# Fourier layer: the middle row by ScalarE and GpSimd, and 64 columns' high and low parts in one stationary operand

## The chip, the cores and the metric

The kernel runs on one core of a Trainium2 chip. A core has a matrix engine (TensorE, PE in the profile, with its weight loads apart as PEld), a vector engine (VectorE, DVE), a scalar engine (ScalarE, ACT), GpSimd (POOL), and DMA queues, most of them fed by SyncE (SP). Each engine works through its own list of instructions in order, and a semaphore holds an instruction back until what it reads is there. Matrix products land in PSUM, in eight banks of 512 fp32 columns; everything else lies in SBUF. The metric is the device time of one execution in microseconds (us), and the median of several runs stands for a kernel.

## The reference

Two equal layers of attention and of Fourier mixing, on 2048 tokens of 640 channels in fp32, 32 heads of 20:

```python
x = A_x
x = x + attention(layernorm(x), wqkv, wo)
x = x + fourier(layernorm(x))
x = x + attention(layernorm(x), wqkv, wo)
x = x + fourier(layernorm(x))

def fourier(x, seq_re, seq_im, hid_re, hid_im):
    a = einsum("bsd,ed->bse", x, hid_re)
    b = einsum("bsd,ed->bse", x, hid_im)
    return einsum("ts,bse->bte", seq_re, a) - einsum("ts,bse->bte", seq_im, b)
```

The matrices are the cosines and sines of the discrete Fourier transforms over 2048 tokens (seq) and 640 channels (hid). Their symmetries let the kernel fold rows and columns: it adds and subtracts mirrored tokens and channels first and then multiplies a quarter of the matrices. Row S/2 of the result, the middle row, falls out of that folding and is computed by itself, with weights of plus and minus one for each token.

## The kernel before

A layer has four stages: QKV projections, the attention sweep (by far the longest), Project, and Fourier. The change touches the last two.

**High and low parts.** A fp32 value is split into a high part in the reduced format fp32r and a low part, the rest (`split`, L85 to L91: the high part by ScalarE, the low part, a subtraction, by VectorE). A product of two such values takes three TensorE passes: high by high, high by low, low by high (`three`, L93 to L98).

**Project** (`Project.run`, L1161) goes over p = 0 to 7, pairs of token tiles. For each p: the output projection (`product`, PSUM tile py, VectorE adds it to the residual xr with a row sum), `moments` (L1104: the mean on GpSimd, squares xsq on ScalarE, then six small GpSimd operations that end in the statistics nb, and VectorE's channel folds g), `scale` (the three ScalarE operations of na, L1133 to L1138) and `normal` (L1144). `normal(p)` multiplies and adds by VectorE (f, L1150); for p = 2, 3, 6, 7 it also folds the tokens by two VectorE operations (L1155) and splits the result into xn, the operand of the Fourier stage, for q = 0, 1, 2, 3 (two tiles each). `LAG` says at which p a `normal(k)` is written: q = 0 at p = 4, q = 1 at p = 5, and q = 2 and 3 behind the last `moments`. There is no planner here: each engine's order is that in which the code is written.

**Fourier** (`Fourier.run`, L1416) makes 16 steps m in the order 0, 1, 4, 5, 2, 6, 3, 7, 8 to 15. `accumulate(m)` multiplies xn (stationary) by the sequence weights chl (moving, 512 columns) into three banks, one for each entry of `FOLDS[ri]`, nine passes in all; step m works on q = m % 4, and ri = (m // 4) % 2 tells the real from the imaginary half. The last step of four may add a three-row corner product (L1308). Then `turn` (L1311) splits the three banks into u. The weights chl are split by `parts` (L1285 to L1296) some steps ahead, in six tiles: those of the steps m = 0, 1, 4, 5, 2 and 6 in Project, those of m = 3, 7, 8, 9 behind the last `normal`, the rest later. `hidden` (L1371) multiplies u by the hidden weights wh, which `weights` (L1211) loads by SP and splits.

**The middle row** (`middle`, L1316). After m = 6 TensorE multiplies the weights mids by xn of q = 0 to 2 (18 passes of 322 or 320 columns into pmid), after m = 7 by q = 3 (6 passes). Three VectorE operations on one partition (L1331, L1333, L1336) bring the sum into um, in the tile c3raw, and add the corner term. After m = 9 six one-column products turn um into columns (pturn), and after m = 10 these are multiplied by the hidden weights.

## Time and profile before

| | us |
|---|---|
| median of 3 runs | 2438.72 (2437.7 to 2438.84) |
| span of the profiled execution | 2438.4 |
| TensorE busy | 2417.5 (99%) |
| ScalarE busy | 2115.4 (87%) |
| VectorE busy | 1008.6 (41%) |
| GpSimd busy | 546.6 (22%) |
| first row of m = 0, second layer, from the span's start | 2361.80 |

The profiled execution has no time of its own beside its span, which lies inside the range of the runs. A row of the trace reads: start in us, length in us, engine, line of the code, operation, the tile written, an arrow, the tiles read, then shapes (partitions x elements), the count, and in brackets how long the engine stood idle before, and what ended that. In the table of stretches the columns behind the window are its length and the busy time of PE, PEld, DVE, ACT and POOL with the number of instructions, then the granted TensorE clock (1.00 is full speed), the DMA engines' busy share and GB/s. TensorE's matmuls are pipelined and overlap, so the distance between two starts is what one costs. The two layers have the same rows here.

### The profile page before, as it was taken

The numbers are of one execution on the slowest core, as the hardware profiler recorded it, in microseconds if no ns is written. First come the engines' busy times: TensorE is split into PE (matmuls) and PEld (weight loads), VectorE is DVE, ScalarE is ACT, GpSimd is POOL, SyncE is SP. The second block draws the span as 40 slices with busy tenths as digits, with TensorE's granted clock in tenths as the row PEclk, the third lists the DMA queues.
The fourth block names the chain that finished last, engine by engine and source line by source line (L and its number), as shares of the span: only waits on it lengthen the run. The fifth ranks groups of instructions, "written<-read, shape, count | busy, mean of one in ns | idle before, by whom it ended". The sixth has DMA issues, their size and how long they took to land. (4 is left out here: it accounts for less than half of the span.)

```text
span 2438.4 us, 43899 instructions
## 1 busy us (share of the span) xinstructions
PE 2417.5 (99%) x16264; PEld 1163.5 (48%) x16264; DVE 1008.6 (41%) x2272; ACT 2115.4 (87%) x2426; POOL 546.6 (22%) x1072
## 2 busy tenths in 40 slices
PE   9999999999999999999999999999999999999998
PEld 8544444543333332339884444454433333333596
DVE  7244442234343333427773444323333232333275
ACT  5699998899999999995457999988999999999862
POOL 3022221112212222115341212211211111222143
PEclk9999999999999999999999999999999999999999
DMA  6324231223222225318573332312221322252265
GB/s 211 121 88 127 84 111 54 77 68 113 72 94 90 88 89 161 102 39 295 187 233 104 108 101 93 110 54 70 82 81 57 92 63 69 57 154 78 76 242 198
DMA packets 130803, 267.88 MB, mean 110 GB/s; under 512 B 30976, under 2 KB 55328, under 8 KB 130580
## 3 DMA queue, kind: packets, MB, share of 16 engines
q1 hardware_dynamic: 90964, 162.51, 20.4%
q0 software_dynamic: 39616, 102.47, 13.3%
q8 instruction: 131, 2.15, 0.4%
q14 instruction: 92, 0.75, 0.1%
HBM read 174.63 MB, written 84.31 MB: 106 GB/s over the span
## 5 line engine op out<-in xcount | busy, mean ns | idle before, releaser
L613 ACT ACTIVATE e<-psc 128x1024 f32<-128x1024 f32 x2048 | 1917.3, 1060 | 108.0 <-PE psc L610 97.7
L621 PE MATMUL acc<-e,v 128*32 128x512 f32 x8192 | 1030.0, 600 | 0.4 <-DVE of L628 0.4
L610 PE MATMUL psc<-stq,stk 62*128 62x512 f32 x4096 | 743.1, 445 | 3.1 <-ACT e L613 2.2
L610 PEld LDWEIGHTS psc<-stq,stk 62*128 62x128 f32 x4096 | 334.5, 184 | 699.7 <-ACT e L613 546.0
L621 PEld LDWEIGHTS acc<-e,v 128*32 128x32 f32 x8192 | 210.2, 108 | 410.8 <-issue 378.1
L103 PE MATMUL pqk<-xt,wqk 128*128 128x512 f32 x1200 | 322.4, 410 | 1.2 <-DVE xt L91 0.7
L642 POOL DMA_DIRECT2D o<-oh x256 | 131.1, 521 | 826.0 <-DVE oh L637 814.3
L88 DVE CAST hl<-pqk 128x512 fp32r<-128x512 f32 x64 | 44.3, 692 | 599.4 <-PE pqk L103 599.4
L103 PEld LDWEIGHTS pqk<-xt,wqk 128*128 128x128 f32 x1200 | 215.1, 189 | 85.6 <-issue 38.0
L103 PE MATMUL pv<-wv,xt 128*128 128x320 f32 x960 | 151.7, 313 | 0.0
L103 PEld LDWEIGHTS pv<-wv,xt 128*128 128x128 f32 x960 | 141.0, 188 | 13.5 <-issue 10.2
L628 DVE STREAM_TRANSPOSE of<-acc 128x512 f32<-128x512 f32 x64 | 45.8, 715 | 225.7 <-PE acc L621 225.7
L642 POOL DMA_DIRECT2D o<-ot x256 | 128.2, 509 | 1.5 <-DVE c L88 0.6
L272 POOL DMA_DIRECT2D scrk<-hl x40 | 28.0, 700 | 398.0 <-DVE hl L91 253.6
L272 POOL DMA_DIRECT2D scrq<-hl x40 | 28.8, 720 | 367.9 <-DVE hl L91 237.6
L96 PE MATMUL py<-wo,o 128*128 128x320 f32 x320 | 101.0, 316 | 0.0
L891 DVE TENSOR_REDUCE far<-cq 128x1 f32<-128x512 f32 (+5 forms) x169 | 98.6, 584 | 5.7
L97 PE MATMUL py<-wo,o 128*128 128x320 f32 x320 | 98.7, 308 | 0.0
L98 PE MATMUL py<-wo,o 128*128 128x320 f32 x320 | 98.7, 308 | 0.0
L895 DVE TENSOR_TENSOR cq<-cq 128x512 f32<-128x512 f32 (+4 forms) x166 | 96.4, 581 | 3.8 <-DMA cq<-in_nat_seq_dram 3.2
L311 DVE COPY v<-pv 128x320 f32<-128x320 f32 x32 | 15.7, 490 | 161.2 <-PE pv L103 161.2
L281 DVE TENSOR_REDUCE top<-pn 32x1 f32<-32x512 f32 x50 | 33.7, 677 | 76.8 <-PE pn L280 76.6
(212 smaller groups left out, 1779.4 us busy)
## 6 DMA issues: line engine op xcount, KB each, us to landing
cq<-in_nat_seq_dram POOLq DMA_DIRECT2D x64, 512.0 KB, 5.2
scrq<-hl POOLq DMA_DIRECT2D x40, 512.0 KB, 3.8
scrk<-hl POOLq DMA_DIRECT2D x40, 512.0 KB, 3.2
stq<-scrq SPq DMA_DIRECT2D x256, 80.0 KB
stk<-scrk SPq DMA_DIRECT2D x128, 160.0 KB
o<-o SPq DMA_DIRECT2D x32, 384.0 KB
stq<-scrq SPq DMA_DIRECT2D x256, 40.0 KB
stk<-scrk SPq DMA_DIRECT2D x128, 80.0 KB
```

The lines of the kernel that those rows point to most:

```text
L96: PE.matmul(out_ap, ah, bh, start=start, stop=False)
L97: PE.matmul(out_ap, ah, bl, start=False, stop=False)
L98: PE.matmul(out_ap, al, bh, start=False, stop=stop)
L103: yield lambda i=i, j=j, k=k: PE.matmul(out_ap, a[i], b[j], start=dc == 0 and k == 0, stop=dc == ND - 1 and k == 2)
L272: G.dma_start(s.scr["qk"[k]][c * 128:(c + 1) * 128, :, tb * 512:(tb + 1) * 512], hl.bitcast(F32))
L610: PE.matmul(p[:, i], s.k[g, kc // 8, j][r, kc % 8 * 128:(kc % 8 + 1) * 128], s.q[g, qb, j][r], start=True, stop=True)
L613: A.activation(e, p, AF.Exp, scale=SCALE)
L621: PE.matmul(s.acc[32 * j:32 * j + 32], s.a.v[kc][:, v0:v0 + 32], s.e[n, j // 2][:, j % 2], start=kc == 0, stop=kc == NT - 1, skip_group_ch ...
L628: V.transpose(t0.rearrange("p b c -> p (b c)"), s.acc)
L642: G.dma_start(s.o[k, h * DH:(h + 1) * DH, qb * 512:(qb + 1) * 512], hl[k][32 * j:32 * j + DH])
L891: V.tensor_reduce(to, x, op=OP.max, axis=AX.X, apply_absolute_value=True)
L895: V.tensor_tensor(y, x, y, op=op)
```

## The change

Three things are changed.

1. The folds of the imaginary half are cut at 449 and 576 in place of 449 and 575, so that the last piece has 64 columns. A tile of xn now holds the high parts of 640 columns, then the low parts with those of the last 64 columns first. The high and the low part of these 64 columns so stand side by side and make one stationary operand of 128 columns (`both`). In the four steps of each half with ri = 1, `accumulate` multiplies it by the high part of chl in one pass into 128 rows, and the high part by chl's low part in a second pass into 64 rows: two passes for three. The corner product of that piece moves ahead of its last pass. The rows of high and low stay apart through `turn`, and `hidden` adds them up over 128 partitions, with the 64 rows of hidden weights loaded twice (two DMAs on SP in place of one). The low part of xn is written by two VectorE operations, of 64 and 576 columns, in place of one.
2. The products of mids and xn after m = 6 and m = 7 are gone. In their place `weigh` stands at the end of `normal`: ScalarE multiplies the two folded tiles of each q by the weight of each partition (321 and 319 columns), and GpSimd adds q = 1, 2 and 3 to the sum (128 x 640). The six one-column products sum over 128 partitions.
3. The corner term of the middle row is added on one partition by one VectorE operation in `edge_sum(1)`, at p = 6; the tile mids is half as large and its split is gone.

The order on ScalarE at the end of Project, where na is that of p = 7, xn and the weighed rows those of q = 3, and chl the weights of m = 3, 7, 8 and 9, stood so before:

```order
L1136 ACTIVATE na<-g,nb,ars 128x321
L1137 ACTIVATE na<-g,nb,ars 128x2
L1138 ACTIVATE na<-g,zero,ars 128x319
L90 ACTIVATE xn<-fold_24675 128x640
L90 ACTIVATE xn<-fold 128x640
L1291 ACTIVATE chl<-craw 128x512 x4
```

and on the same engine at the same place it now reads:

```order
L1137 ACTIVATE na<-g,nb,ars 128x321
L1138 ACTIVATE na<-g,nb,ars 128x2
L1139 ACTIVATE na<-g,zero,ars 128x319
L1161 ACTIVATE xn<-fold_24675 128x640
L1161 ACTIVATE xn<-fold 128x640
L1286 ACTIVATE c3raw<-fold_24675,zero,mid 128x321
L1286 ACTIVATE c3raw<-fold,zero,mid 128x319
L1317 ACTIVATE chl<-craw 128x512 x4
```

The two weighing operations of q = 3 stand between xn and the four chl; those of q = 0, 1 and 2 stand behind their xn in the same way.

On GpSimd, between p = 4 and p = 5 (nb are the statistics of p = 4, mean and sumsq those of p = 5), the order was:

```order
L1128 TENSOR_TENSOR nb<-ars 128x1
L1129 TENSOR_SCALAR nb<-nb 128x1
L1130 TENSOR_SCALAR nb<-ars 128x1
L1110 TENSOR_TENSOR mean<-rowsum 128x2
L1111 TENSOR_SCALAR mean<-mean 128x2
L1115 TENSOR_SCALAR sumsq<-sumsq 128x2
```

and on GpSimd it now is:

```order
L1129 TENSOR_TENSOR nb<-ars 128x1
L1130 TENSOR_SCALAR nb<-nb 128x1
L1131 TENSOR_SCALAR nb<-ars 128x1
L1290 TENSOR_TENSOR um<-um 128x640
L1111 TENSOR_TENSOR mean<-rowsum 128x2
L1112 TENSOR_SCALAR mean<-mean 128x2
L1116 TENSOR_SCALAR sumsq<-sumsq 128x2
```

The addition of q = 1 stands ahead of the mean of p = 5. Those of q = 2 and 3 stand behind nb of p = 7, where GpSimd had nothing until `hidden`.

On TensorE, from the last passes of m = 6 to the first of m = 3, there stood (the line of dots leaves out 16 more passes into pmid):

```order
L96 MATMUL pacc<-chl,xn 65x512
L97 MATMUL pacc<-chl,xn 65x512
L98 MATMUL pacc<-chl,xn 65x512
L96 MATMUL pmid<-xn,mids 66x322
...
L98 MATMUL pmid<-xn,mids 66x320
L96 MATMUL pacc<-chl,xn 128x512
```

and TensorE now has there:

```order
L99 MATMUL pacc<-chl,xn 127x512
L1332 MATMUL pacc<-chl,xn 128x512
L1334 MATMUL pacc<-chl,xn 64x512
L97 MATMUL pacc<-chl,xn 128x512
L98 MATMUL pacc<-chl,xn 128x512
```

The first pass of m = 3 comes right behind the two passes of m = 6's last piece.

```diff
@@ -33,7 +33,8 @@
 HD = D // 2
 TOL = 2.0 ** -32
 
-FOLDS = (((0, 128), (128, 128), (256, 65)), ((321, 128), (449, 126), (575, 65)))
+FOLDS = (((0, 128), (128, 128), (256, 65)), ((321, 128), (449, 127), (576, 64)))
+WIDE = (1, 2)
 
 
 @with_exitstack
@@ -1032,7 +1033,7 @@
     class Project:
         def __init__(s, att, src, dst):
             s.att, s.src, s.dst, s.w, s.raw = att, src, dst, {}, {}
-            s.sum = {}
+            s.sum, s.both = {}, {}
             s.oh, s.x, s.xn, s.rs, s.f, s.g, s.nb, s.na = {}, {}, {}, {}, {}, {}, {}, {}
 
             s.begun, s.parts = set(), [lambda n=n, i=i: s.begin(n, i) for n in range(5) for i in range(2)]
@@ -1154,9 +1155,14 @@
             for k, op in enumerate((OP.add, OP.subtract)):
                 V.tensor_tensor(t[k], s.f[p - 2], f, op=op)
             for k in range(2):
-                xn = s.next.keep(f"xn{2 * q + k}", [2, D], F32R, "xn")
-                s.xn[q, k] = [xn[:, 0], xn[:, 1]]
-                split(xn[:, 0], xn[:, 1], t[k])
+                xn = s.next.keep(f"xn{2 * q + k}", [2 * D], F32R, "xn")
+                cut = FOLDS[1][2][0]
+                s.xn[q, k], s.both[q, k] = [xn[:, :D], xn[:, 2 * D - cut:]], xn[:, cut:]
+                A.activation(xn[:, :D], t[k], AF.Copy)
+                for to, cols in ((D, slice(cut, D)), (2 * D - cut, slice(cut))):
+                    V.tensor_tensor(xn[:, to:to + cols.stop - (cols.start or 0)], t[k][:, cols],
+                                    xn[:, cols].bitcast(F32), op=OP.subtract)
+            s.next.weigh(q, t)
 
         def run(s):
             s.ot[2] += s.heads(s.room, 2, (1,))
@@ -1208,6 +1214,10 @@
             s.loads = [0, 2, 1] + list(range(3, 8))
             pr.next = s
 
+        @staticmethod
+        def deep(ri, c):
+            return FOLDS[ri][c][1] * (2 if (ri, c) == WIDE else 1)
+
         def weights(s, k):
             ri, c = divmod(k, 3)
             k0, n = FOLDS[ri][c]
@@ -1216,11 +1226,12 @@
                 s.w[ri, c] = s.late(f"wh{k}", [2, HD + 2], F32R, "wh")
                 s.raw["w", k] = s.late(f"raw{(k + 1) % 2}", [D], F32, "whraw")[:, :HD + 2]
                 r0 = k0 - HD * ri
-                nc.sync.dma_start(s.raw["w", k][:n], hid[ri, r0:r0 + n, :HD + 2])
+                for a in range(0, s.deep(ri, c), n):
+                    nc.sync.dma_start(s.raw["w", k][a:a + n], hid[ri, r0:r0 + n, :HD + 2])
 
             def parts():
-                w = s.w[ri, c]
-                split(w[:n, 0], w[:n, 1], s.raw["w", k][:n], vector=True)
+                w, d = s.w[ri, c], s.deep(ri, c)
+                split(w[:d, 0], w[:d, 1], s.raw["w", k][:d], vector=True)
 
             return load, parts
 
@@ -1260,14 +1271,29 @@
                 A.activation(h, e, AF.Copy)
                 return
             V.tensor_tensor(l, e, h.bitcast(F32), op=OP.subtract)
+            m = s.um[0:1, :HD + 1]
+            V.scalar_tensor_tensor(m, e[:, :HD + 1], s.mm[0:1, 0:1], m, op0=OP.mult, op1=OP.add)
             nc.sync.dma_start(s.e3[1:2, 0].bitcast(F32), h.bitcast(F32))
             nc.sync.dma_start(s.e3[2:3, 0].bitcast(F32), l.bitcast(F32))
 
+        def weigh(s, q, t):
+
+            if q == 0:
+                x = s.keep("xn7", [2, D], F32, "um")
+                s.um, s.term = x[:, 0], x[:, 1]
+            to = s.room[:, :D] if q == NQ - 1 else s.term if q else s.um
+            for ri, cols in enumerate((slice(0, HD + 1), slice(HD + 1, D))):
+                A.activation(to[:, cols], t[ri][:, cols], AF.Identity, scale=s.midraw[:, ri, q // 2, q % 2:q % 2 + 1],
+                             bias=zero)
+            if q:
+                um = s.um if q == 1 else to if q == NQ - 1 else s.pr.room("xsq", [D], F32, "um")
+                G.tensor_tensor(um, s.um, to, op=OP.add)
+                s.um = um
+
         def mids(s):
-            x = s.keep("mids", [4, 80], F32R, "mids")
+            x = s.keep("mids", [2, 80], F32R, "mids")
             V.memset(x.bitcast(F32), 0.0)
-            s.mid, s.uc = [x[:, 0], x[:, 1]], [x[:, 2], x[:, 3]]
-            split(s.mid[0][:, :8], s.mid[1][:, :8], s.midraw.rearrange("p r k i -> p (r k i)"), vector=True)
+            s.uc = [x[:, 0], x[:, 1]]
 
 
         ORDER = (0, 1, 4, 5, 2, 6, 3, 7) + tuple(range(8, 16))
@@ -1301,44 +1327,39 @@
                 s.acc[ri] = [bank(f"b{3 * ri + c}", [128, 512], "pacc") for c in range(3)]
             ch, last = s.c[m], q == NQ - 1
             for c, (k0, n) in enumerate(FOLDS[ri]):
-                three(s.acc[ri][c][:n], [x[:, k0:k0 + n] for x in s.pr.xn[q, ri ^ tb]], (ch[:, 0], ch[:, 1]),
-                      q == 0, last and ri != tb)
+                x, stop = s.pr.xn[q, ri ^ tb], last and ri != tb
+                if (ri, c) == WIDE:
+                    fs = [lambda first, end: PE.matmul(s.acc[ri][c], s.pr.both[q, ri ^ tb][:, :2 * n], ch[:, 0],
+                                                       start=first, stop=end),
+                          lambda *_: PE.matmul(s.acc[ri][c][:n], x[0][:, k0:k0 + n], ch[:, 1], start=False, stop=False)]
+                    if last and ri == tb:
+                        fs.append(lambda *_: s.corner(tb, ri, c, False))
+                    for f in fs[::-1] if last else fs:
+                        f(q == 0, last)
+                else:
+                    three(s.acc[ri][c][:n], [y[:, k0:k0 + n] for y in x], (ch[:, 0], ch[:, 1]), q == 0, stop)
             if last and ri == tb:
-                for c, (k0, n) in enumerate(FOLDS[ri]):
-                    PE.matmul(s.acc[ri][c][:n], s.e3[0:3, 0, k0:k0 + n], s.c3[0:3, tb * 512:(tb + 1) * 512],
-                              start=False, stop=True)
+                for c in range(3):
+                    if (ri, c) != WIDE:
+                        s.corner(tb, ri, c, True)
+
+        def corner(s, tb, ri, c, stop):
+            k0, n = FOLDS[ri][c]
+            PE.matmul(s.acc[ri][c][:n], s.e3[0:3, 0, k0:k0 + n], s.c3[0:3, tb * 512:(tb + 1) * 512], start=False, stop=stop)
 
         def turn(s, tb, ri):
             u = s.u[tb, ri] = [s.own(f"u{(4 * tb + 2 * ri + k) % 6}", [3, 512], F32R, "u") for k in range(2)]
-            for c, (_, n) in enumerate(FOLDS[ri]):
+            for c in range(3):
+                n = s.deep(ri, c)
                 split(u[0][:n, c], u[1][:n, c], s.acc[ri][c][:n])
 
         def middle(s, step):
 
             if step == 0:
-                s.um = s.room[0:1, :2 * HD + 2]
-                s.pm = [bank(f"b{6 + ri}", [128, 512], "pmid")[:66] for ri in range(2)]
-            if step < 2:
-                for ri, (k0, n) in enumerate(((0, HD + 2), (HD, HD))):
-                    p = s.pm[ri][:, :n]
-                    for q in (range(NQ - 1), (NQ - 1,))[step]:
-                        j = NQ * ri + q
-                        three(p, [s.mid[k][:, j:j + 66] for k in range(2)],
-                              [x[:, k0:k0 + n] for x in s.pr.xn[q, ri]], q == 0, q == NQ - 1)
-                    if step == 0:
-                        continue
-                    if ri == 0:
-                        V.scalar_tensor_tensor(s.um[:, :HD + 1], s.e3[0:1, 0, :HD + 1].bitcast(F32), s.mm[0:1, 0:1],
-                                               p[0:1, :HD + 1], op0=OP.mult, op1=OP.add)
-                        V.scalar_tensor_tensor(s.um[:, :HD + 1], s.e3[0:1, 1, :HD + 1].bitcast(F32), s.mm[0:1, 0:1],
-                                               s.um[:, :HD + 1], op0=OP.mult, op1=OP.add)
-                    else:
-                        V.tensor_copy(s.um[:, HD + 1:D], p[0:1, 1:])
-            elif step == 2:
                 p = bank("b6", [128, 6], "pturn")
                 for ri in range(2):
                     for c, (k0, n) in enumerate(FOLDS[ri]):
-                        PE.matmul(p[:n, 3 * ri + c:3 * ri + c + 1], s.um[:, k0:k0 + n], one[0:1], start=True, stop=True)
+                        PE.matmul(p[:n, 3 * ri + c:3 * ri + c + 1], s.um[:, k0:k0 + n], one, start=True, stop=True)
                 for ri in range(2):
                     for c, (_, n) in enumerate(FOLDS[ri]):
                         i = 3 * ri + c
@@ -1377,7 +1398,8 @@
             if t == NQ and s.dst is out:
                 s.end(0)
             for ri in range(2):
-                for c, (_, n) in enumerate(FOLDS[ri]):
+                for c in range(3):
+                    n = s.deep(ri, c)
                     three(p[ri], [s.u[t // NQ, ri][k][:n, c, o:o + 128] for k in range(2)],
                           [s.w[ri, c][:n, k] for k in range(2)], c == 0, c == 2)
                 if final:
@@ -1429,8 +1451,8 @@
                     s.parts(i + s.AHEAD)
                 elif i >= NQ + 2:
                     s.parts(i + s.AHEAD - 2)
-                if m in (6, 7, 9, 10):
-                    s.middle((6, 7, 9, 10).index(m))
+                if m in (9, 10):
+                    s.middle(m - 9)
                 if 11 <= m < 14:
                     s.hidden(m - 11)
                 if m == 13:
```

## The prediction

> **What bounds the kernel now.** I read the page first, then TensorE by stretches, then the records of each engine around the place where Project hands over to Fourier. Times below are those of the second layer; the first layer's rows are the same ones 1207.31 us earlier.
>
> ```profile
> span 2438.4 us, 43899 instructions
> PE 2417.5 (99%) x16264; PEld 1163.5 (48%) x16264; DVE 1008.6 (41%) x2272; ACT 2115.4 (87%) x2426; POOL 546.6 (22%) x1072
> ...
> 2370.00:2387.00 17.00, 17.00 (x82) 12.69 (x81) 13.34 (x22) 9.67 (x19) 0.99 (x1) 1.00 0.61 223
> ```
>
> TensorE is busy for 99% of the span and for all 17 us of the stretch that the change touches, at clock 1.00 (the number behind POOL's). Whatever is taken off it there is gained, up to the point where it must wait for an operand. So two questions decide: how much TensorE work goes, and when its next operand is there. TensorE's own rows (start, length; lengths overlap, so the pitch between starts is the cost):
>
> ```profile
> 2372.28 0.40 PE L96 MATMUL pacc<-chl,xn 128*128 128x512 f32 x1
> 2372.51 0.39 PE L97 MATMUL pacc<-chl,xn 128*128 128x512 f32 x1
> ...
> 2374.38 0.31 PE L96 MATMUL pmid<-xn,mids 128*66 128x322 f32 x1
> ...
> 2377.03 0.40 PE L96 MATMUL pacc<-chl,xn 128*128 128x512 f32 x1
> 2377.26 0.40 PE L97 MATMUL pacc<-chl,xn 128*128 128x512 f32 x1
> ...
> 2382.28 0.31 PE L96 MATMUL pmid<-xn,mids 128*66 128x322 f32 x1
> ...
> 2383.16 0.39 PE L96 MATMUL pacc<-chl,xn 128*128 128x512 f32 x1
> ```
>
> The first pair is step m=6 (nine passes, pitch 0.233 us), then come 18 middle-row passes, m=3 (its first two passes shown), its corner products and m=7, six more middle-row passes, m=8.
>
> The records of ScalarE (ACT), VectorE (DVE) and GpSimd (POOL) that feed m=3, with what ended an idle time in brackets:
>
> ```profile
> 2368.72 0.67 POOL L1129 TENSOR_SCALAR nb<-nb 128x1 f32<-128x1 f32 x1
> 2369.35 0.20 POOL L1130 TENSOR_SCALAR nb<-ars 128x1 f32<-128x1 f32 x1
> ...
> 2369.42 0.66 ACT L1136 ACTIVATE na<-g,nb,ars 128x321 f32<-128x321 f32 x1 [0.99 <-POOL nb L1129]
> 2370.41 0.64 ACT L1138 ACTIVATE na<-g,zero,ars 128x319 f32<-128x319 f32 x1
> 2372.59 1.60 ACT L90 ACTIVATE xn<-fold 128x640 fp32r<-128x640 f32 x2 [1.55 <-DVE fold L1155]
> 2374.10 2.18 ACT L1291 ACTIVATE chl<-craw 128x512 fp32r<-128x512 f32 x4
> ...
> 2370.60 0.55 DVE L1150 SCALAR_TENSOR_TENSOR fold<-g,ars,na 128x321 f32<-128x321 f32 x1 [1.30 <-ACT na L1137]
> 2371.73 1.68 DVE L1155 TENSOR_TENSOR fold<-fold 128x640 f32<-128x640 f32 x2
> 2373.37 1.69 DVE L91 TENSOR_TENSOR xn<-fold,xn 128x640 fp32r<-128x640 f32 x2
> 2374.97 2.49 DVE L1293 TENSOR_TENSOR chl<-craw,chl 128x512 fp32r<-128x512 f32 x4
> ```
>
> This is one chain: GpSimd's last statistics (nb), ScalarE's na, VectorE's two fold steps, the last xn, and behind it the four chl tiles, of which the first is m=3's. Its low half ends near 2375.65 (the four take 2.49 with their overlap, so some 0.68 for one), and m=3's second pass, the first to need it, starts at 2377.26. So the 18 middle-row passes stand exactly where TensorE would otherwise wait: the slack is 1.61 us.
>
> **The change, part by part.** *TensorE.* The 18 passes take 2377.03 − 2374.38 = 2.65 us, the six take 0.88. Eight of the sixteen steps lose one pass of 0.233. Ahead of m=3 that is m=4, 5 and 6: 0.70 + 2.65 = 3.35 us. Behind it it is m=7 and m=12 to 15 and the six passes: 1.17 + 0.88 = 2.05. If nothing waited, 5.39 us a layer, 10.8 in all. The new operand's 128 columns, the 127-row tiles, the hidden weights' second DMA on SP and the six 1-column products over 128 partitions I cost at nothing: passes of 65 and 128 output rows above have the same pitch, and the weights' transfers lie far ahead. Their bound the other way is some tenths.
>
> *Behind m=3* the 2.05 us should arrive whole in the second layer. The first layer ends otherwise: there VectorE's moments stand ahead of the last turn and run into it without an idle,
>
> ```profile
> 1209.24 0.16 DVE L131 TENSOR_SCALAR ars<-amv 128x2 f32<-128x2 f32 x1
> 1209.31 1.88 DVE L91 TENSOR_TENSOR u<-pacc,u 128x512 fp32r<-128x512 f32 x3
> ```
>
> so that m=14 and m=15 (0.47) may bring nothing. Between 1.58 and 2.05 I take 1.7.
>
> *ScalarE.* Two weighing operations stand behind each of the four xn pairs; the nearest rows have the same shape (na, 0.66 and 0.64, overlapping by a tenth), 1.1 us. Behind the last pair they hold up m=3's chl by 1.1.
>
> *GpSimd.* Three additions of 640 columns a layer. No row has the shape; the nearest are
>
> ```profile
> 2407.74 0.74 POOL L1368 TENSOR_TENSOR xs<-xs,c3raw 1x321 f32<-1x321 f32 x1
> ...
> 2405.06 0.87 POOL L1368 TENSOR_TENSOR xd<-xd,r 128x321 f32<-128x321 f32 x1 [2.06 <-issue]
> ...
> 2404.84 0.48 DVE L1368 TENSOR_TENSOR xd<-xd,r 128x321 f32<-128x321 f32 x1
> 2405.24 1.04 DVE L1369 TENSOR_TENSOR xd<-xd,r 128x319 f32<-128x319 f32 x1
> ```
>
> 321 columns alone take 0.74, so I take 1.4 for 640 (bounds 0.9, and 2.2 from the 1.1 that the contended half costs). The last two rows show the price to VectorE: an addition of 0.48 becomes 1.04 when GpSimd's is under way, as if it stood until GpSimd's had ended. [...]
>
> *The first addition* stands on GpSimd between the statistics of p=4 and the mean of p=5, and waits for the second weighing. What waits behind it:
>
> ```profile
> 2348.35 0.19 POOL L1110 TENSOR_TENSOR mean<-rowsum 128x2 f32<-128x2 f32 x1
> ...
> 2346.72 1.60 ACT L90 ACTIVATE xn<-fold 128x640 fp32r<-128x640 f32 x2 [2.26 <-DVE fold L1155]
> 2350.26 0.82 ACT L1113 ACTIVATE xsq<-xr,mean 128x640 f32<-128x640 f32 x1
> 2354.72 0.66 ACT L1136 ACTIVATE na<-g,nb,ars 128x321 f32<-128x321 f32 x1 [2.07 <-POOL nb L1130]
> 2360.09 0.66 ACT L1136 ACTIVATE na<-g,nb,ars 128x321 f32<-128x321 f32 x1 [1.98 <-POOL nb L1129]
> 2362.58 0.43 POOL L1110 TENSOR_TENSOR mean<-rowsum 128x2 f32<-128x2 f32 x1 [2.36 <-DVE xr L1095]
> 2363.55 0.83 ACT L1113 ACTIVATE xsq<-xr,mean 128x640 f32<-128x640 f32 x1 [1.83 <-POOL mean L1111]
> 2366.83 1.60 ACT L90 ACTIVATE xn<-fold 128x640 fp32r<-128x640 f32 x2 [1.41 <-DVE fold L1155]
> ```
>
> xn ends near 2348.3, the weighing at 2349.4, the addition, with VectorE's folds in the way, near 2351.3, the mean of p=5 near 2352.3 in place of 2349.3. ScalarE's xsq of p=5 then starts about 2 us late, and na of p=5 and p=6 some 2.8 late. The mean of p=7 waited 2.36 us for the products (rowsum, from VectorE's xr), not for this chain, so of the 2.8 only 1.0 is left at xsq of p=7, and its statistics end 0.7 late: na of p=7 starts near 2370.1.
>
> [...] m=3's second pass starts at 2378.65 where it was 2377.26: 1.39 later, in place of up to 3.35 earlier. The two-piece low part of xn costs VectorE about 0.1 each and hides under ScalarE's chl.
>
> *The clock.* TensorE is out of work at 2373.67 (2377.03 less 3.35) and gets one pass near 2377.0, then waits to 2378.65. Rows on what such a gap does (length, TensorE's busy time, and behind POOL's its clock):
>
> ```profile
> 10.35:13.77 3.42, 1.71 (x9) 1.03 (x9) 2.67 (x4) 3.42 (x8) 0.73 (x16) 1.00 1.00 357
> 13.77:17.19 3.42, 3.42 (x10) 2.64 (x9) 3.42 (x8) 2.68 (x7) 0.00 (x0) 0.50 1.05 388
> ...
> 1219.39:1220.37 0.98, 0.31 (x4) 0.04 (x2) 0.55 (x2) 0.44 (x1) 0.98 (x2) 1.00 1.02 408
> 1220.37:1223.80 3.43, 3.43 (x26) 3.21 (x27) 3.02 (x7) 2.56 (x5) 3.15 (x5) 1.00 0.96 313
> ...
> 2430.40:2433.80 3.40, 0.00 (x0) 0.00 (x0) 0.00 (x0) 0.00 (x0) 0.00 (x0) 0.50 0.64 229
> ```
>
> A half-idle 3.42 us was followed by 3.42 us at half clock; an idle second was not. A gap of 3.4 + 1.4 us is nearer to the first. If the clock falls around 2377.1 for 3.42 us, 1.85 us of it is work, which loses 0.9. Bounds: 0 and 1.7 (a whole window of work).
>
> *The sum.* m=3: +1.39 twice. Behind it: −2.05 and −1.7. Clock: +0.9 twice. Together 2.78 − 3.75 + 1.8 = +0.8 us on a span of 2438.4, a change no larger than the spread of the runs. The profiled execution is 0.3 us below the median of 2438.72, so on that footing the changed kernel takes **2439.6 us**. A measurement of this kernel tells a difference of about 0.2% (4.9 us) from none.
>
> **Rivals.** *(a) The same waits, no fall of the clock.* The gap might count as two gaps. [...] Without it: 2439.6 − 1.8 = 2437.8.
>
> *(b) Faster: GpSimd's additions find gaps.* If they hold VectorE nowhere and the first one's delay is absorbed in the 1.4 to 2.1 us idles of the rows above, only the last weighing counts: m=3's low half ends at 2375.65 + 1.1 − the 0.2 VectorE was behind, near 2376.5, 0.75 earlier than now: 2 × −0.75 − 3.75 = −5.3, 2433.5. With the weighing hidden too, −1.6 a layer: 2431.8. All 10.8 us (2427.9) would need chl of m=3 by 2374, before the last xn is even done; the chain excludes it nearly.
>
> *(c) Slower: the first addition's delay reaches the end of the chain.* If it comes later or contended (2.2 us), statistics of p=7 end 3 us late and not 0.7: m=3's second pass falls to 2381, 3.7 late. 2 × 3.7 − 3.75 = +3.7, with a clock window of 0.9 to 1.7 each: 2444 to 2446. It decides from the point where the second pass starts later than about 2379.1 less the clock's loss (2377.26 + 1.9 a layer is the break-even). For it: four idles in the rows name GpSimd as releaser. Against it: the 2.36 us in which the mean of p=7 waits for TensorE's products resets the lag.
>
> **How the numbers follow.** My forecast with the clock's fall 0.38, (a) 0.25, (b) 0.15, (c) 0.22. Of (b) some two thirds end below 2433.8 with a few tenths of doubt from the unpriced parts; of (c) nearly all end above 2443.6, and a little of the forecast does when the clock costs its upper bound twice. So faster 0.12, within 0.2% 0.63, slower 0.25. The range leaves out the ends of (b) and (c): 2432.5 to 2446.
>
> **What would show it.** Of the forecast: no pmid rows from xn; a TensorE idle of 4 to 5 us before and inside the start of m=3, released by ScalarE's or VectorE's chl; VectorE's fold step of p=7 or its first chl low part drawn out beside a GpSimd addition of about 1.4; clock below 1.00 in the stretch after the idle. (b) shows as an idle under 3 us, (c) as one over 7 or as idles before m=2 and m=6 too. I am wrong if the additions are far from 1.4 us, or if the chain of p=5 to p=7 has more or less slack than its idles say.

## The result, and the profile after

The changed kernel takes 2445.7 us (median of 5 runs, 2443.83 to 2449.05), the kernel before 2438.62 (2437.7 to 2438.84). By the medians it is 7.1 us slower, by more than the 0.2% that tell a difference; the ratio worked out over all runs is 1.0033, with a 95% interval of 1.0021 to 1.0046. The time lies in the stated range, near its upper end, but the forecast of no change was wrong; what came is the path of rival (c), by another cause than it named.

The head of the changed kernel's page, TensorE's waits over the whole span (us in total, times, longest) and the stretch around the hand-over of the second layer:

```profile
span 2443.8 us, 43813 instructions
PE 2412.2 (99%) x16200; PEld 1156.5 (47%) x16200; DVE 1011.8 (41%) x2280; ACT 2123.9 (87%) x2442; POOL 560.6 (23%) x1078
...
PE pacc L97 <- ACT chl L1317: 8.4, 2, 4.2
...
PE pacc L98 <- DVE chl L1319: 1.8, 2, 0.9
...
2370.00:2387.00 17.00, 11.66 (x40) 7.24 (x38) 11.95 (x19) 10.27 (x20) 5.77 (x9) 0.80 0.18 62
```

TensorE has 5.3 us less work and waits for m=3's chl twice, once a layer, 4.2 us for the high half and 0.9 for the low one. In the stretch where it was busy for 17.00 us it is now busy for 11.66, at a mean clock of 0.80. The rows below are of the second layer. It begins 2.59 us later than before: from one layer's m=0 to the other's 4.34 us were lost, but the first m=0 came 1.75 us earlier in this execution, mostly because the one profiled before had its clock at half for 3.4 us at 85.5, and this one had not:

```profile
2376.53 0.40 PE L1334 MATMUL pacc<-chl,xn 128*64 128x512 f32 x1
2381.14 0.80 PE L97 MATMUL pacc<-chl,xn 128*128 128x512 f32 x1 [4.21 <-ACT chl L1317]
2382.85 0.79 PE L98 MATMUL pacc<-chl,xn 128*128 128x512 f32 x1 [0.92 <-DVE chl L1319]
2383.45 0.63 PE L99 MATMUL pacc<-chl,xn 128*128 128x512 f32 x1
2383.87 0.63 PE L97 MATMUL pacc<-chl,xn 128*128 128x512 f32 x1
```

m=6 ends, m=3's first pass comes 4.6 us later, its second at 2382.85, that is 2380.26 on the time axis of before, where it stood at 2377.26. The passes that follow stand 0.42 apart in place of 0.233. The stretches around them, cut where the clock changes, show it (the number behind POOL's):

```profile
1164.22:1167.63 3.41, 1.03 (x5) 0.46 (x3) 3.34 (x6) 1.48 (x3) 0.24 (x1) 1.00 0.00 0
1167.63:1174.46 6.83, 4.06 (x9) 2.46 (x9) 4.58 (x7) 3.36 (x7) 1.54 (x1) 0.50 0.34 112
2375.96:2379.37 3.41, 0.97 (x5) 0.40 (x3) 3.34 (x6) 1.50 (x3) 0.15 (x1) 1.00 0.00 0
2379.37:2386.19 6.82, 4.13 (x9) 2.46 (x9) 4.50 (x7) 3.27 (x7) 1.54 (x1) 0.50 0.30 109
```

In each layer the clock is at half for 6.8 us, the later half of it with work. Upstream, GpSimd and ScalarE of the changed kernel:

```profile
2352.09 1.92 POOL L1290 TENSOR_TENSOR um<-um 128x640 f32<-128x640 f32 x1 [0.85 <-ACT um L1286]
...
2357.38 0.54 POOL L1116 TENSOR_SCALAR sumsq<-sumsq 128x2 f32<-128x2 f32 x1 [1.99 <-ACT xsq L1114]
...
2361.57 0.21 POOL L1131 TENSOR_SCALAR nb<-ars 128x1 f32<-128x1 f32 x1
...
2361.64 0.66 ACT L1137 ACTIVATE na<-g,nb,ars 128x321 f32<-128x321 f32 x1 [3.83 <-POOL nb L1130]
2368.16 0.66 ACT L1137 ACTIVATE na<-g,nb,ars 128x321 f32<-128x321 f32 x1 [3.12 <-POOL nb L1130]
2369.70 0.81 ACT L1114 ACTIVATE xsq<-xr,mean 128x640 f32<-128x640 f32 x1
2374.46 0.66 ACT L1137 ACTIVATE na<-g,nb,ars 128x321 f32<-128x321 f32 x1 [0.43 <-POOL nb L1130]
2380.47 2.17 ACT L1317 ACTIVATE chl<-craw 128x512 fp32r<-128x512 f32 x4
```

The first addition starts at 2352.09 and takes 1.92. ScalarE then waits 3.83 us for the statistics of p=5 and 3.12 for those of p=6, where it had waited 2.07 and 1.98. With 2.59 taken off, na of p=5 is 4.3 us late, na of p=6 5.5, xsq of p=7 3.6, na of p=7 2.45 and chl of m=3 3.8. VectorE beside the additions:

```profile
2351.76 0.82 DVE L1125 TENSOR_TENSOR g<-xr 128x638 f32<-128x638 f32 x1
2352.49 2.20 DVE L1126 TENSOR_TENSOR g<-xr 128x638 f32<-128x638 f32 x1
...
2381.11 3.49 DVE L1319 TENSOR_TENSOR chl<-craw,chl 128x512 fp32r<-128x512 f32 x4 [0.71 <-ACT chl L1317]
```

One fold of 0.82 became 2.20 beside the first addition, and the four low parts of chl, 2.49 before, took 3.49 beside the third.

### The profile page after: what moved, and what is told of

It reads as the page before. It is cut to its first block, busy times and chain, and to the rows that moved or that the text cites. A ratio compares the mean times of both kernels' runs of the same rounds, so it can differ in the third digit from the quotient of the medians.

```text
span 2443.8 us, 43813 instructions
## 1 busy us (share of the span) xinstructions
PE 2412.2 (99%) x16200; PEld 1156.5 (47%) x16200; DVE 1011.8 (41%) x2280; ACT 2123.9 (87%) x2442; POOL 560.6 (23%) x1078
## 5 line engine op out<-in xcount | busy, mean ns | idle before, releaser
L104 PEld LDWEIGHTS pv<-wv,xt 128*128 128x128 f32 x960 | 141.0, 188 | 13.4 <-issue 10.2
```

The source lines that it names most:

```text
L104: yield lambda i=i, j=j, k=k: PE.matmul(out_ap, a[i], b[j], start=dc == 0 and k == 0, stop=dc == ND - 1 and k == 2)
```

## The experiments

All rows below are of the second layer's profile, in us from its first row of m=0, so that what happened earlier cancels. The column of half clock tells how long the clock stood at half around m=3, in the first and the second layer. In the first layer m=3's second pass lies within 0.02 us of the figure shown, but for two runs: 15.60 without additions and 14.79 without a middle row.

| kernel | m=3, second pass | m=7 | pturn | half clock | median (kernel before, beside it) | ratio, 95% interval |
|---|---|---|---|---|---|---|
| before | 15.46 | 18.30 | 25.63 | none | 2438.6 | |
| changed | 18.46 | 22.92 | 29.05 | 6.8, 6.8 | 2445.7 (2438.6) | 1.0033 (1.0021 to 1.0046) |
| new operand only | 14.79 | 17.62 | 24.77 | none | 2435.8 (2438.7) | 0.9991 (0.9981 to 1.0000) |
| middle row only | 18.54 | 23.10 | 29.51 | 6.8, 6.8 | 2448.7 (2438.7) | 1.0044 (1.0027 to 1.0061) |
| first addition later | 17.17 | 22.11 | 28.24 | 10.2, 6.8 | 2446.4 (2438.7) | 1.0031 (1.0020 to 1.0042) |
| no additions | 14.83 | 17.75 | 23.89 | 3.4, none | 2438.3 (2438.7) | 0.9998 (0.9988 to 1.0008) |
| gap filled | 18.47 | 21.39 | 27.52 | none | 2442.3 (2439.1) | 1.0011 (1.0001 to 1.0020) |
| first addition later, gap filled | 17.16 | 20.08 | 26.21 | none | 2439.9 (2439.1) | 1.0004 (0.9994 to 1.0014) |
| chl ahead of the last weighing | 16.66 | 21.14 | 27.28 | 3.4, 3.4 | 2444.6 (2439.1) | 1.0025 (1.0015 to 1.0034) |
| reordered | 12.05 | 15.35 | 22.71 | none | 2433.1 (2439.1) | 0.9974 (0.9962 to 0.9985) |
| reordered, sum last | 12.05 | 15.34 | 21.47 | none | 2431.2 (2438.6) | 0.9978 (0.9968 to 0.9987) |
| no middle row | 14.03 | 18.71 | 26.15 | none, 6.8 | 2436.5 (2438.6) | 0.9994 (0.9985 to 1.0004) |

**The two parts apart.** The new operand with the middle row on TensorE as before (the new lines of `middle`, which take the low parts where the new layout has them):

```diff
...
+                         fs = [lambda a, z: PE.matmul(p, mh, h[:, k0:k0 + n], start=a, stop=z),
+                               lambda *_: PE.matmul(p, ml, h[:, k0:k0 + n], start=False, stop=False),
+                               lambda *_: PE.matmul(p[:, :w], mh, l[:, k0:k0 + w], start=False, stop=False)]
+                         if w < n:
+                             fs.append(lambda *_: PE.matmul(p[:, w:], mh, s.pr.both[q, ri][:, 64:128], start=False, stop=False))
...
```

> Theory C (the chain): the loss comes from the first GpSimd addition, which stands ahead of the mean of p=5 and makes every statistic from p=5 to p=7 late, so that m=3 waits; the new stationary operand itself only saves TensorE passes. Rival E (end of the chain): the loss comes from the last weighing and the last two additions, behind nb of p=7. Rival P (passes): the new operand costs something itself. This kernel has the new operand with the middle row on TensorE as before (the low parts of the last 64 columns take four short passes of their own a layer). C and E: 16 passes of 0.233 us less 0.35 for the first layer's end and some 0.5 for the short passes, 2435.5 to 2436.3 against 2438.6, no wait ahead of m=3. P: 2438 or more.

and the middle row by ScalarE and GpSimd with the old operand (against the kernel before):

```diff
                 split(xn[:, 0], xn[:, 1], t[k])
+            s.next.weigh(q, t)
...
-                if m in (6, 7, 9, 10):
-                    s.middle((6, 7, 9, 10).index(m))
+                if m in (9, 10):
+                    s.middle(m - 9)
```

> The middle row by ScalarE and GpSimd as in the changed kernel, the operand as before with three passes. C and E: as slow as the changed kernel and more, since m=3 waits just the same and the passes of m=7 and m=12 to 15 come back (2 x 1.17): 2447 to 2449. P: the loss goes with the new operand, 2435 to 2439.

2435.84 and 2448.73, both as forecast. Rival P falls: the operand costs nothing by itself, and its median is 2.8 us lower, though the interval of its ratio touches 1. Its 0.67 us at m=3's second pass (15.46 to 14.79) are the 0.70 of m=4, 5 and 6, and no wait stands ahead of m=3. The whole loss is the middle row's.

**Which of its steps.** The first addition moved behind nb of p=6:

```diff
-            if q:
-                um = s.um if q == 1 else to if q == NQ - 1 else s.pr.room("xsq", [D], F32, "um")
+            if q > 1:
+                um = to if q == NQ - 1 else s.pr.room("xsq", [D], F32, "um")
...
+        def add_late(s):
+            G.tensor_tensor(s.um, s.um, s.term, op=OP.add)
...
                     s.next.edge_sum(1)
+                    s.next.add_late()
```

> The changed kernel with the first GpSimd addition moved behind nb of p=6, where GpSimd stood idle for 2.4 us before, and the corner term added to the sum ahead of it. C: xsq of p=5 starts within 0.7 us of where it did before, nb of p=7 ends no later than 0.5 us, m=3's second pass comes near 1 us late in place of 3, 2436 to 2440. E: m=3 stays 2.5 us late or more, 2443 to 2446.

and no additions at all:

```diff
             if q:
-                um = s.um if q == 1 else to if q == NQ - 1 else s.pr.room("xsq", [D], F32, "um")
-                G.tensor_tensor(um, s.um, to, op=OP.add)
-                s.um = um
+                s.um = to
```

> The changed kernel without the three GpSimd additions of a layer: the middle row's sum is left out (the term of the last q alone goes on), so the middle row is not that of the reference. Only ScalarE's weighing stays. C: m=3's second pass near 2376.6 on the time axis of before, 0.7 early, 2433 to 2436. E: if the weighing on ScalarE is what counts, 2441 or more; if the last two additions are, 2433 to 2436 too, but then the run with the first addition moved stays slow.

Where m=3's second pass stands takes the lateness of 3.0 us apart (second layer). Moving the first addition takes 1.3 of it (18.46 to 17.17), taking all three away 3.6 (to 14.83). The last two additions stand behind nb of p=7, so they cannot delay na of p=7. It starts 2.45 us late in the changed kernel and 0.05 late without additions: 2.4 of the 3.6 come by the first addition, 1.2 by the last two. In its new place the first addition still costs 1.1, since it stands ahead of the mean of p=7 and beside a VectorE step that took 0.55 before. Rows of GpSimd and VectorE of that run:

```profile
2366.29 1.57 POOL L1295 TENSOR_TENSOR um<-um 128x640 f32<-128x640 f32 x1
2367.82 0.44 POOL L1111 TENSOR_TENSOR mean<-rowsum 128x2 f32<-128x2 f32 x1
...
2366.62 1.60 DVE L1151 SCALAR_TENSOR_TENSOR fold<-g,ars,na 128x321 f32<-128x321 f32 x1
```

So both theories held a part: neither C's chain nor E's end alone. C had also said 0.7 us at xsq of p=5 and 0.5 at nb of p=7. It was 1.1 at both: at xsq by the weighing, since it is 1.1 without additions as well, and at nb by the moved addition.

The times did not follow these rows. Without additions 2433 to 2436 was expected, and 2438.3 came, as before the change. In the first layer of that run the mean of p=5 came 1.4 us later than in the second, which the rows leave open, m=3's second pass was 0.14 late, and the clock was at half for 3.4 us. With the first addition moved m=3 came 1.3 us earlier, but the kernel was no faster, 2446.4, where C said 2436 to 2440. Its stretches, with the clock behind POOL's column:

```profile
1165.67:1169.08 3.41, 0.50 (x1) 0.19 (x1) 2.67 (x6) 3.23 (x6) 1.27 (x1) 1.00 0.00 0
1169.08:1179.32 10.24, 9.36 (x21) 5.99 (x22) 6.23 (x10) 4.20 (x9) 0.95 (x2) 0.50 0.82 297
```

Both are of the first layer: the clock stayed at half for 10.2 us, and TensorE had work in 9.36 of them. An earlier operand put more work into the slow windows. That made the clock the next suspect.

**The clock by itself.** Products that nobody reads, in the gap ahead of m=3, in the changed kernel (28) and in the one with the first addition moved (23):

```diff
+                if m == 6:
+                    p = bank("b6", [128, 512], "pfill")[:66, :HD]
+                    for k in range(28):
+                        PE.matmul(p, s.uc[0][:, :66], s.pr.xn[k % 3, 0][0][:, :HD], start=k == 0, stop=k == 28 - 1)
```

> The changed kernel with 28 products of 320 columns, 4.1 us, into an unused bank in TensorE's idle time ahead of m=3; nothing reads them. Theory H (half clock): the fall of the clock over the idle, two windows of 3.4 us of which about 3 us are work, costs some 1.6 us a layer beside the wait itself; with TensorE busy the clock stays at 1.00, m=3's passes go back from 0.43 to 0.233 us, and the time falls from 2445.7 to 2441.5 to 2443.5. Theory W (the wait alone): the loss is the late operand, the clock changes little, 2445 to 2447.

> The run with the first addition moved behind nb of p=6, with 23 such products, 3.4 us, ahead of m=3. There m=3's second pass was 1.7 us late in place of 3.0, but the clock stayed at half for three windows in the first layer and two in the second, over work that was ready. H: without the fall of the clock the earlier operand shows: 2438 to 2440.5, against 2446.4. W: 2444 or more.

The changed kernel with the gap filled, TensorE's rows at m=3 and the stretch:

```profile
2379.40 0.50 PE L97 MATMUL pacc<-chl,xn 128*128 128x512 f32 x1 [0.19 <-ACT chl L1317]
2381.12 0.51 PE L98 MATMUL pacc<-chl,xn 128*128 128x512 f32 x1 [1.22 <-DVE chl L1319]
2381.46 0.39 PE L99 MATMUL pacc<-chl,xn 128*128 128x512 f32 x1
2381.70 0.39 PE L97 MATMUL pacc<-chl,xn 128*128 128x512 f32 x1
...
2379.30:2386.10 6.80, 5.48 (x21) 3.52 (x22) 5.28 (x7) 4.03 (x9) 1.22 (x1) 1.00 0.58 205
```

Nothing of the wait has changed (18.47, and 18.46 without the products), but the clock is 1.00, the passes stand 0.24 apart, and m=7 comes 1.53 us sooner (22.92 to 21.39). The medians fell by 3.4 us, 1.7 a layer, to 2442.3; H had said 2441.5 to 2443.5. Beside it the moved addition shows what it is worth: 2439.9, in H's 2438 to 2440.5. Without the fall of the clock the changed kernel would lose 3.2 us and not 7.1.

**The end of the chain.** m=3's chl ahead of the last weighing; `begin` holds m=0's products and then the split of m=3's chl:

```diff
+            if q == NQ - 1:
+                s.next.begin()
             s.next.weigh(q, t)
```

> The changed kernel with m=3's chl split ahead of the last weighing (and m=0's products written ahead of it, whose tile it takes). The weighing of q=3 and the last addition then stand behind what m=3 needs. E (end of the chain): m=3's second pass comes 1.1 us earlier by ScalarE and up to 1 more since VectorE's low part meets no addition, and the gap of TensorE shrinks from 6 to about 4 us with one window at half clock in place of two: 2440 to 2443. C alone (the chain ahead of nb of p=7): 1.1 us a layer, 2443 to 2445.

m=3's second pass came 1.8 us earlier (16.66), of the 1.1 to 2.1 that E gave, the gap had one slow window a layer, and m=7 came 1.8 earlier. The profiled execution was 2.6 us faster for it (2443.03 against 2445.61), the median only 1.1, 2444.6: E's time was missed though its rows came, and the time alone fits C. The runs go from 2441.9 with a mean clock of 0.997 to 2448.7 with 0.994, so some seem to have more slow windows than the profiled one.

**No middle row at all.** A zeroed tile in its place:

```diff
-            s.next.weigh(q, t)
...
-            V.scalar_tensor_tensor(m, e[:, :HD + 1], s.mm[0:1, 0:1], m, op0=OP.mult, op1=OP.add)
...
+            s.um = s.room[:, :D]
+            G.memset(s.um, 0.0)
```

> The changed kernel with no middle row's sum at all: no weighing, no additions, no corner term; a zeroed tile takes its place, so the middle row is not that of the reference. It tells what the slack of m=3 is worth with nothing added to ScalarE, VectorE or GpSimd. By the reading of the profile before (low part of m=3's chl at 2375.65, second pass at 2377.26) m=3 can only come 1.5 us earlier a layer of the 3.35 us taken off, TensorE idles near 1.5 to 2 us ahead of it, and the clock stays: 2431 to 2433. If the chain has more slack than that, towards 2428; if the short idle already lowers the clock, 2433 to 2436.

m=3's second pass at 14.03 is 1.43 earlier than before in the second layer: there the slack was read rightly (1.5). In the first layer it is only 0.67 earlier; the mean of p=5 is late there as in the run without additions. The median is 2436.5 in place of 2431 to 2433, just above the 2433 to 2436 given for a fall of the clock, and the runs go from 2433.1 to 2442.9. Their mean granted clock goes with the time: 0.999 and 0.998 in the two fastest, 0.994 in the two slowest. TensorE's rows at m=3 in the second layer of the profiled execution, then two stretches of the first layer and three of the second. Their ends lie whole steps of 3.413 us from 2373.26, as the seven changes of the clock in the changed kernel's profile do from one another (13.93, 17.34, 1167.63, 1174.46, 2379.37, 2386.19 and 2437.39), so they are, by this estimate, the points at which the clock could change:

```profile
2371.53 0.49 PE L97 MATMUL pacc<-chl,xn 128*128 128x512 f32 x1 [1.06 <-ACT chl L1302]
2372.54 0.50 PE L98 MATMUL pacc<-chl,xn 128*128 128x512 f32 x1 [0.52 <-DVE chl L1304]
...
1161.54:1164.95 3.41, 2.35 (x11) 1.48 (x9) 3.33 (x6) 1.74 (x3) 0.00 (x0) 1.00 0.00 0
1164.95:1168.36 3.41, 2.14 (x8) 1.45 (x9) 3.41 (x7) 2.27 (x5) 0.00 (x0) 1.00 0.19 41
...
2369.85:2373.26 3.41, 1.84 (x7) 0.95 (x6) 3.41 (x8) 3.07 (x6) 0.00 (x0) 1.00 0.00 0
2373.26:2376.67 3.41, 3.41 (x10) 1.77 (x8) 1.03 (x2) 0.20 (x1) 0.00 (x0) 0.50 0.83 300
2376.67:2380.09 3.42, 3.42 (x9) 2.19 (x8) 2.99 (x5) 2.48 (x5) 0.00 (x0) 0.50 0.98 326
```

In the second layer idles of 1.06 and 0.52 us were enough: the clock fell after they were over. From m=3's second pass to pturn this layer took 12.12 us and the first 9.05, so the fall cost 3.07, more than the 1.43 gained. In the first layer a longer gap, idles of 1.81 and 0.52 us, cost nothing. There it is divided between two stretches, which left TensorE busy for 2.35 and 2.14 us; in the second layer it lies in one, with 1.84. Where a gap lies on this grid so seems to count; no run tests it. Busy time alone does not decide: in the kernel before TensorE was busy for 2.31 us both in the stretch from 82.04, after which the clock fell, and in that from 1290.36, after which it did not.

**Both parts, in another order.** The weighings were put where ScalarE had idled, the additions where GpSimd had, and the chl of m=3 and m=7 ahead of the end of the chain (`begin` here holds the products of m=0 and m=1 and then these two splits, `last_sum` two additions):

```diff
+                if p in (4, 5):
+                    s.next.weigh(p - 4)
...
                     s.next.edge_sum(1)
+                    s.next.first_sum()
...
-            for k in (NP - 2, NP - 1):
-                s.normal(k)
+            s.normal(NP - 2)
+            s.next.begin()
+            s.scale(NP - 1)
+            s.next.weigh(2)
+            s.normal(NP - 1)
+            s.next.weigh(3)
+            s.next.last_sum()
```

> Both parts of the change, in another order: the weighings of q=0 and 1 behind xsq of p=4 and p=5, that of q=2 behind na of p=7 and that of q=3 behind the last xn, in idle times that ScalarE had before; the first addition behind the corner term at p=6, the other two behind the last weighing; chl of m=3 and m=7 split ahead of na of p=7, with m=0 and m=1 written ahead of them. If waits and the clock that follows from them are the whole loss, m=3 waits for next to nothing and the removed 10.8 us show nearly whole: 2428 to 2431, clock 1.00. If the work itself on ScalarE, VectorE and GpSimd is too much for that stretch, m=3 still waits 1 us or more: 2432 to 2438.

2433.1 (ratio 0.9974) beats both kernels, but misses the 2428 to 2431. m=3 waits for next to nothing; m=8 now does. Rows of GpSimd, VectorE and TensorE of that run:

```profile
2374.68 3.55 POOL L1306 TENSOR_TENSOR c3raw<-c3raw,um 128x640 f32<-128x640 f32 x2 [5.46 <-ACT um L1297]
...
2375.15 3.63 DVE L1334 TENSOR_TENSOR chl<-craw,chl 128x512 fp32r<-128x512 f32 x2 [0.72 <-ACT chl L1332]
2378.70 1.87 DVE L92 TENSOR_TENSOR u<-pacc,u 128x512 fp32r<-128x512 f32 x3
...
2379.43 0.50 PE L97 MATMUL pacc<-chl,xn 128*128 128x512 f32 x1 [0.97 <-DVE u L92]
```

The two chl, 1.3 us alone, took 3.63 beside the additions, u's low parts came late behind them, and m=8 with them. So the additions were moved once more, behind the products of m=4 and m=5 and the splits of m=8's and m=9's chl:

```diff
             s.next.weigh(3)
+            s.next.begin(2, 3)
...
         def last_sum(s):
+            G.tensor_copy(s.midraw[:, 0, 0, 0:1], s.c[s.ORDER[9]][:, 1, 0:1].bitcast(F32))
```

> The reordered run with its last two additions moved once more: the chl of m=8 and m=9 are split first, and GpSimd reads one column of them before it adds, so that the additions meet VectorE's low parts of u, which read PSUM and one tile, and no chl. In the reordered run VectorE's two chl took 3.6 us in place of 1.3 beside the additions, and m=8 waited 0.97 us for the low part of u in each layer. If that is an exclusion by instructions with two SBUF inputs, the wait goes: 2 us less than the reordered run, 2430.5 to 2432. If GpSimd's additions hold up any VectorE work, u's low parts are drawn out in their turn and the time stays: 2432.5 to 2434.

The same instructions on GpSimd and VectorE in that run, and TensorE's stretch:

```profile
2370.71 3.86 POOL L1309 TENSOR_TENSOR c3raw<-c3raw,um 128x640 f32<-128x640 f32 x2
...
2369.20 1.29 DVE L1337 TENSOR_TENSOR chl<-craw,chl 128x512 fp32r<-128x512 f32 x2 [0.72 <-ACT chl L1335]
2370.65 1.88 DVE L92 TENSOR_TENSOR u<-pacc,u 128x512 fp32r<-128x512 f32 x3
...
2370.00:2387.00 17.00, 16.91 (x88) 12.95 (x87) 11.45 (x25) 9.20 (x21) 7.11 (x6) 1.00 0.70 262
```

The chl are back at 1.29, u's low parts run undisturbed beside the additions (1.88, as before), TensorE is busy for 16.91 of 17 us, and the median is 2431.17, as said, the lowest of all: 7.4 us under the kernel before and 14.5 under the changed one, with both parts of the change in it. So the additions drew out the two chl that they met in the reordered run, which read two SBUF tiles (3.63 in place of 1.29), and not u's low parts, which read PSUM and one SBUF tile (1.88).

The rows show what the last move is worth (pturn comes 1.24 us earlier, and m=8 no longer waits); the times do not tell the two orders apart, since the intervals of their ratios overlap. The profiled execution is the fastest of ten. The others go up to 2438.5, and the mean granted clock from 0.998 down to 0.995, so this order too seems to have slow windows in some runs, and no trace shows where.

## Why the prediction was wrong, point by point

**What TensorE loses, and the slack of m=3: right.** Of the 10.8 us taken off the page shows 5.3 less busy time, since the passes that the clock slowed are in it too; the new operand alone brings the 0.70 ahead of m=3, and without any middle row m=3 came 1.43 us sooner in the second layer, where 1.5 to 1.6 of slack was read. That ScalarE's, GpSimd's and VectorE's work would turn the gain ahead of m=3 into a wait was right as well.

**The first addition: its place and length right, its reach wrong.** It started within 0.1 us of the forecast 2349.4 (2352.09 − 2.59 = 2349.5) and took 1.92. The step that failed is the next one: "of the 2.8 only 1.0 is left at xsq of p=7, and its statistics end 0.7 late". Measured were 3.6 and 2.45. The run without additions shows that this is the first addition's doing: there xsq of p=7 starts where it did before, and na of p=7 0.05 late. I had carried the delay on with the old lengths of GpSimd's small operations, but a delayed step falls beside other VectorE work. Statistics of p=5, from sumsq to the last nb, before:

```profile
2352.21 0.19 POOL L1115 TENSOR_SCALAR sumsq<-sumsq 128x2 f32<-128x2 f32 x1 [2.90 <-ACT xsq L1113]
...
2354.20 0.48 POOL L1130 TENSOR_SCALAR nb<-ars 128x1 f32<-128x1 f32 x1
```

They took 2.5 us, beside VectorE's evictions from PSUM; in the changed kernel 4.4 (2357.38 to 2361.78), beside folds, g and chl. That the neighbours make the difference is read from the rows and not tested. It could have been read ahead: the same operations of p=7, beside folds and xn, took 4.0 us in the kernel before (2365.51 to 2369.55). The lag grew from 2.6 at xsq of p=5 to 5.5 at na of p=6, and the 2.36 us that the mean of p=7 used to wait for TensorE were used up: it started 3.1 us late, behind nb of p=6.

**The second and third addition.** I had, by estimate, 0.5 us for the second, beyond the 0.7 that na was late, and 0.9 for the third; no run shows these figures. In the changed kernel the second cost VectorE's fold only 0.3 (0.82 in place of 0.55), since na of p=7 was later still, and the third drew the low parts of chl out by 1.0.

**m=3 in sum: 1.39 late was forecast, 3.0 came.** Twice, that is 3.2 us of the error. No run shows the 1.39, nor the first pass near 2377.0 and the second at 2378.65 behind it: they rest on these two estimates and on the 0.7. In the changed kernel the two passes came at 2378.55 and 2380.26 on that axis.

**The clock: the fall was right, its price too low.** 0.9 a layer was forecast for one window, with m=3's second pass at the 2378.65 that no run shows; two windows came, and the filled run puts their price at 1.5 by the rows and 1.7 by the medians. It is 1.2 to 1.6 us of the error. In the 3.41 us before the falls TensorE was busy for 1.03 and 0.97 us in the changed kernel and for 1.84 without a middle row. The slow times around m=3 were 3.4, 6.8 and 10.2 us long.

**Behind m=3: sized too high.** 2.05 and 1.7 were forecast. The six passes of the middle row and m=7's pass came (from m=7 to pturn 6.13 us with the gap filled, 7.33 before). But from pturn to the last hidden product the changed kernel needs 38.8 us in the second layer, 39.2 before, and 39.4 against 39.3 in the first: of the 0.93 of m=12 to 15 0.4 was kept in one layer and nothing in the other. The gain behind m=3 was 2.7 us in all, 1 less than forecast. In the first layer a hidden product waits 0.28 us for VectorE's u, of the kind that the forecast had for half of that; what took the rest is open.

**The sum.** With the measured terms, 6.0 + 3.2 − 2.7 = 6.5 of the 7.1 us. The other 0.6 I cannot place. My footing was off as well: an execution's time is 1.8 us above its span (2445.61 and 2443.8), so the profiled execution before was not 0.3 under the median but, if that holds for it too, 1.5 above. The half clock at 85.5 us, which the changed kernel's execution does not have, fits this.

**The rivals.** (c) had the right path, a delay that reaches the end of the chain, but not the cause: it had the first addition come later or take 2.2 us, and it came on time and took 1.92. Its 2444 to 2446 came partly by luck: m=3's second pass was at 2380.26 and not at 2381 (1.5 us less in two layers), which the smaller gain behind m=3 made up by 1 us. I gave it 0.22 because of the wait of p=7's mean, which took 2.4 us off the lag (from 5.5 to 3.1) but did not end it. (a) fell: in the changed kernel the clock went to half at 2379.37, ahead of the pass that breaks the gap (2381.14), and without a middle row it did so behind a gap that a pass breaks (idles of 1.06 and 0.52 us). (b) could not be had in this order; with another order more than it was, since chl of m=3 need not stand behind the last xn, which I had taken as given.

## What to carry to other kernels

Work put on an idle engine is not free if it stands in the order ahead of a step of a chain: count the queue behind it, and price the delayed steps anew, beside what they will now meet, not by their old lengths. Passes taken off a full TensorE ahead of a late operand become a gap (here idles of 4.21 and 0.92 us), and a gap of one or two us can cost more than its length by the clock (without a middle row a fall of the clock behind idles of 1.06 and 0.52 us cost 3.07), so first get the operand earlier (here by splitting it ahead of the chain's end), then take the passes away. By the medians the same two-part change was 7 us slower in one order and 7 us faster in another.

## What the hardware showed that I had not expected

- Idles of 1.06 and 0.52 us, with TensorE busy for 1.84 of the 3.41 us in which they lay, were followed by 6.8 us at half clock; a longer gap in the other layer of the same execution was not. Runs of one program lay 5 to 10 us apart (2443.8 to 2449.1 changed, 2433.1 to 2442.9 without a middle row, 2429.2 to 2438.5 with the sum last), and the slowest had a lower mean clock than the fastest (0.994 and 0.995 changed, 0.994 and 0.999 without a middle row, 0.995 and 0.998 with the sum last). The kernel before stayed within 1.1 in its first five runs and within 5.2 in the 23 beside the first experiments.
- What ends half clock is open. Two slow stretches of 3.41 us that TensorE filled were followed by another slow one, those from 2373.26 without a middle row and from 1172.49 with the first addition later. Both hold more than 1 us of the corner products, which have three rows; the slow stretches that ended half clock around m=3 hold at most 0.74. No run tests this.
- Products that nobody reads, put in a gap, made the kernel faster by 3.4 us (2445.7 to 2442.3) without changing when m=3's second pass came (18.46 and 18.47).
- A single GpSimd addition of 640 columns took 1.54 to 1.57 us where VectorE was idle (1.56 and 1.54 at 2374.55 and 2380.71 of the changed kernel) or read PSUM (1.57 at 2366.29 with the first addition later) when it began, and 1.92 where it was in a fold of two SBUF inputs (at 2352.09 of the changed kernel). The next fold, also of two SBUF inputs, took 2.20 in place of 0.82 and ended 0.68 after that addition. Of u's low parts, which read PSUM, three together took 1.88 beside the additions, as before; a chl of two SBUF inputs between two such groups took 0.68 there, as in the kernel before (at 2350.60), while the two additions took 3.86.
